# Sliding-window attention and a channel mix on one core: instruction order from a list scheduler, and another order of the first loads

## The chip, the cores and the metric

The kernel runs on one core of one Trainium2 chip. The metric is the device time of one execution in microseconds (us). Each kernel is executed several times and once with the hardware profiler on; "the profile" and "the trace" are of that profiled execution, whose span is about 1.7 us shorter than the device time of the same run. TensorE is called PE below, and its weight loads PEld; VectorE, ScalarE, GpSimd and SyncE appear in the profile as DVE, ACT, POOL and SP.

## The reference

Eight batches of eight heads, 576 positions, 64 channels per head. Attention over a window of 128 positions with a linear distance bias, then a gated two-layer channel mix on the 512 channels. Cut to what matters:

```python
scores = scale * (q @ k.T)                       # per batch and head
mask   = (rel >= 0) & (rel < 128)                # rel = query position - key position
attn   = softmax(where(mask, scores - slope[h] * abs(rel), -1e9))
x      = concat_heads(attn @ v)                  # [8, 576, 512]
xk, xr = mixes of x and x shifted by one position
k      = relu(xk @ w_k) ** 2                     # 512 -> 1024
out    = sigmoid(xr @ w_r) * (k @ w_v)           # 1024 -> 512
```

Note the first matmul of the mix: it sums over all 512 channels, so it needs the attention of all four head pairs for its positions before it can start.

## The kernel before

Work goes by head pair: 32 pairs (8 batches of 4). For one pair PE transposes Q and K, computes the scores, multiplies with V and transposes the result; ScalarE copies the transposes out of PSUM and takes the exponent; VectorE divides by the sums and forms `xk` and `xr`. The channel mix comes in blocks of up to 512 positions, whose pieces ("units") fill PE between the attention steps. The order of the instructions is written by hand (from batch 2 on for PE, SyncE and GpSimd alone; ScalarE and VectorE are then not in the hand-ordered set).

The distance bias can be applied in two ways. For the first two batches (`NEARLY = 2 * G` head pairs) PE adds it into the scores with an extra matmul; later VectorE multiplies the exponent by a mask that was made meanwhile.

```python
    def scores(it, pieces, m0):
        early = it < NEARLY                       # NEARLY = 2 * G: batches 0 and 1
        ...
        if early:
            for hl in range(2):
                nc.tensor.matmul(sa[:, hl, 0:w], lhsT=sid[:, 2 * g + hl],
                                 rhs=dist[:, m0:m0 + w], start=True, stop=False, ...)
        ...                                       # scores, then exp on ScalarE
        if not early:
            nc.vector.tensor_tensor(out=ah, in0=ah,
                in1=mask[:, 2 * g:2 * g + 2, m0:m0 + w], op=ALU.mult)
```

Batch 0 is loaded in two halves of 256 positions in f32 by SyncE and cast on GpSimd, VectorE and ScalarE. The weights follow from GpSimd, which casts while loading, then batch 1:

```python
    load_qk(0, 1, 0); load_qk(1, 1, 0); load_v_block(0, 0); ...   # batch 0, f32, SyncE
    ...
    for i in range(2 * G):                        # i < G: first half of pair i, then second halves
        score(i)
        ...
        if i == G - 1:
            load_w(wk_sb, moe_w_k)
            load_w(wr_sb, moe_w_r)
            load_w(wv_sb, moe_w_v)
        ...
    cast_load_qk(1, 0); cast_load_qk(1, 1); cast_load_tail(1); cast_load_v(1)
    ...
    def first1(c0, fo):                           # first layer of the mix, 256 positions
        mm1(0, c0, c0 + 256, fo)
        if c0 == 256:
            make_mask(range(fo, fo + 1))
```

The softmax here doesn't subtract the row's maximum and nothing guards it: scores larger than these inputs give would overflow.

## Time and profile before

| | before |
|---|---|
| time, median (range) | 266.53 us of the first three runs (266.39 to 267.29) |
| span of the profiled run | 264.8 us |
| PE busy | 239.7 us, 91% |
| first score matmul, first matmul with w_k | 5.24 us, 28.73 us |
| batch 1's first transposes, batch 2's first scores | 40.40 us, 66.61 us |

The head of the page of the kernel before: span, busy time by engine, then the busy share of PE in 40 equal slices in tenths (9 is 90% or more).

```profile
span 264.8 us, 5798 instructions
PE 239.7 (91%) x2272; PEld 144.2 (54%) x2304; DVE 190.1 (72%) x406; ACT 180.0 (68%) x293; POOL 102.9 (39%) x147
PE   4489799977999999999999999999999999999993
```

PE is the busiest engine, and the holes are nearly all in the first ten slices (66 us). But busy is not progress: a matmul at the half clock, or one that stands in the pipeline behind a slow one, counts as busy. The same shows in the table of windows (start and end, length, busy us and instructions of PE, PEld, VectorE, ScalarE, GpSimd; then granted clock, DMA share, GB/s):

```profile
0.00:20.00 20.00, 11.74 (x93) 5.73 (x94) 7.80 (x31) 10.60 (x19) 12.32 (x38) 0.99 0.99 199
20.00:60.00 40.00, 35.56 (x399) 22.14 (x401) 25.48 (x63) 30.96 (x58) 34.32 (x43) 0.96 2.14 165
30.00:40.00 10.00, 9.10 (x70) 6.47 (x69) 6.61 (x21) 7.78 (x24) 6.19 (x8) 1.00 2.25 162
60.00:240.00 180.00, 172.07 (x1680) 105.27 (x1702) 148.39 (x294) 129.03 (x198) 56.26 (x68) 1.00 0.86 90
```

The marks of progress on PE, from the timeline of the kernel before (start, duration, engine, line, operation, output and inputs, count, and in brackets the idle time ahead with what ended it):

```profile
5.24 0.50 PE L242 MATMUL sa<-qk 64*128 64x256 bf16 x4
15.78 0.75 PE L209 MATMUL tp<-ident,cs 128*128 128x128 bf16 x4
28.73 2.34 PE L324 MATMUL ps<-xk,wk_sb 128*128 128x256 bf16 x16
40.40 0.61 PE L196 MATMUL tp<-ident,ldr 128*128 128x128 bf16 x8
```

The first scores start at 5.24 us, the second half of batch 0 at 15.78, the channel mix at 28.73, batch 1 at 40.40. And GpSimd, which issues the casting loads:

```profile
17.23 0.91 POOL L404 DMA_DIRECT2D wv_sb<-in_moe_w_v_dram  x1
32.56 0.87 POOL L110 DMA_DIRECT2D ldr<-in_k_dram  x1 [3.62 <-DMA wv_sb<-in_moe_w_v_dram]
```

The load of w_v is issued at 17.23 us, and GpSimd stands 3.62 us for it before it may issue the last K load of batch 1.

**A count of progress.** I need a measure that does not count slow time as work. I give each matmul its time at full speed, from the trace: 0.216 us for 512 columns (back to back in the steady state), 0.1625 for 384, 0.109 for 256, 0.056 for a 128-column transpose, 0.029 for one of 65 (or 64) columns, and half for the score matmuls of 64 rows, which run in pairs side by side (the two of a pair start 3 to 4 ns apart). Summed over the weight loads, whose records are complete where some matmul records are missing, this is 218.6 us for the kernel before. "Lost" up to a moment is the elapsed time less the work started by then. The kernel before has lost 14.7 us by 20 us, 25.4 by 60, 41.2 by 240 and 46.2 at the end. This is bookkeeping of mine, not a view of the profile.

### The profile page before, as it was taken

The page shows a single profiled execution, that of the slowest core. Times are in us where ns is not written, and L with a number is a line of the kernel's source. Part 1 is how long each engine was busy: PE and PEld are TensorE (multiplying, and loading weights), DVE is VectorE, ACT ScalarE, POOL GpSimd, SP SyncE. Part 2 cuts the span into 40 slices and gives each one's busy share as a digit, 9 for nine tenths or more (in the row PEclk, how much of TensorE's full clock was granted, in tenths as well). Part 3 has the DMA queues.
Part 4 walks back from the last instruction along what each step waited for, and adds up shares of the span by engine and source line. Part 5 has one row for each costly group of instructions (what it writes and reads, how often), then busy time and mean ns, then how long its engine had stood idle before and what let it go on. Part 6 is the DMA issues. An engine that isn't in the chain of part 4 may idle for free.

```text
span 264.8 us, 5798 instructions
## 1 busy us (share of the span) xinstructions
PE 239.7 (91%) x2272; PEld 144.2 (54%) x2304; DVE 190.1 (72%) x406; ACT 180.0 (68%) x293; POOL 102.9 (39%) x147
## 2 busy tenths in 40 slices
PE   4489799977999999999999999999999999999993
PEld 1145664544555755555665755555656655555461
DVE  2259952379758988878887788878778889886241
ACT  5368688873886877876786868866766868626250
POOL 6399389999048066606470249314000000000000
PEclk9997999999999999999999999999999999999999
DMA  6999999999939897939995299919201111031212
GB/s 163 239 197 188 189 155 143 170 144 178 141 23 157 122 87 108 143 57 92 125 145 70 82 129 106 115 42 146 66 30 51 41 42 40 2 119 41 79 42 80
DMA packets 115788, 28.38 MB, mean 107 GB/s; under 512 B 105008, under 2 KB 110640, under 8 KB 115760
## 3 DMA queue, kind: packets, MB, share of 16 engines
q0 software_dynamic: 100608, 15.02, 83.1%
q1 hardware_dynamic: 15152, 12.98, 16.4%
q8 instruction: 18, 0.29, 0.5%
q14 instruction: 10, 0.08, 0.1%
HBM read 33.56 MB, written 9.44 MB: 162 GB/s over the span
## 4 chain that ended last, share of the span: by engine, by line
PE 60%; ACT 13%; DMA 11%; DVE 7%; issue 3%; POOL 3%; SPq 1%; POOLq 0%; DVEq 0%; ACTq 0%
PE pv L353 20%; PE ps L324 16%; PE pr L339 10%; ACT at L245 6%; DMA wv_sb<-in_moe_w_v_dram 6%; PE sa L274 5%; PE tp L196 4%; ACT xt L301 3%; DMA ts<-in_k_dram 3%; DMA vdr<-in_v_dram 2%; PE sa L242 2%; ACT rl L328 2%; PE tp L296 2%; DVE xk L312 2%; ACT qk L199 1%
## 5 line engine op out<-in xcount | busy, mean ns | idle before, releaser
L324 PE MATMUL ps<-xk,wk_sb 128*128 128x256 bf16 (+2 forms) x413 | 70.4, 313 | 2.4 <-ACT rl L328 1.5
L245 ACT ACTIVATE at<-sa 128x1024 bf16<-128x1024 f32 (+1 forms) x68 | 63.7, 984 | 8.0 <-PE sa L242 7.7
L353 PE MATMUL pv<-wv_sb,kk 128*128 128x512 bf16 x271 | 67.7, 379 | 1.2 <-issue 0.5
L328 ACT ACTIVATE rl<-ps 128x256 bf16<-128x256 f32 (+2 forms) x104 | 47.6, 477 | 18.3 <-PE ps L324 13.6
L324 PEld LDWEIGHTS <-wk_sb 128*128 128x128 bf16 x416 | 38.6, 98 | 23.3 <-issue 4.0
L330 DVE TENSOR_TENSOR kk<-rl 128x256 bf16<-128x256 bf16 (+2 forms) x104 | 33.6, 337 | 16.6 <-ACT rl L328 14.4
L116 POOL DMA_DIRECT2D vs<-in_v_dram x28 | 24.8, 908 | 42.4 <-PE sa L274 41.3
L359 DVE SCALAR_TENSOR_TENSOR ot<-rs,pv 128x512 f32<-128x512 bf16 x36 | 24.4, 678 | 23.1 <-PE pv L353 17.5
L353 PEld LDWEIGHTS <-kk 128*128 128x128 bf16 x288 | 26.0, 98 | 26.3 <-DVE kk L330 0.4
L344 ACT ACTIVATE rs<-pr 128x512 bf16<-128x512 f32 x36 | 21.7, 602 | 23.9 <-PE pr L339 23.9
L339 PE MATMUL pr<-wr_sb,xr 128*128 128x512 bf16 x132 | 35.7, 379 | 0.7
L199 ACT COPY qk<-tp 128x1024 bf16<-128x1024 bf16 x28 | 28.4, 1015 | 10.9 <-PE tp L196 10.6
L110 POOL DMA_DIRECT2D ldr<-in_q_dram x28 | 25.1, 917 | 24.3 <-PE tp L196 24.3
L247 DVE TENSOR_TENSOR at<-at,mask 128x1024 bf16<-128x1024 bf16 x48 | 31.0, 684 | 0.8 <-ACT at L245 0.8
L274 PEld LDWEIGHTS <-at 128*128 128x128 bf16 x576 | 22.6, 99 | 12.0 <-issue 7.5
L312 DVE SCALAR_TENSOR_TENSOR xk<-dl,muk_sb,xt 128x576 bf16<-128x576 bf16 (+2 forms) x36 | 27.1, 752 | 1.2
L310 DVE TENSOR_TENSOR dl<-xt 128x576 bf16<-128x576 bf16 (+2 forms) x36 | 15.5, 431 | 16.2 <-ACT xt L301 15.6
L312 DVE SCALAR_TENSOR_TENSOR xr<-dl,mur_sb,xt 128x576 bf16<-128x576 bf16 (+2 forms) x36 | 26.9, 748 | 0.0
L110 POOL DMA_DIRECT2D ldr<-in_k_dram x28 | 24.8, 924 | 4.4 <-DMA wv_sb<-in_moe_w_v_dram 3.6
L282 DVE TENSOR_TENSOR xu<-sa,rc 128x640 bf16<-128x640 f32 x28 | 22.9, 820 | 0.5
L274 PE MATMUL sa<-vs,at 128*128 128x65 bf16 x448 | 18.9, 193 | 3.0 <-ACT at L245 2.6
L242 PE MATMUL sa<-qk 64*128 64x256 bf16 (+1 forms) x264 | 20.8, 265 | 0.6 <-ACT qk L212 0.2
(61 smaller groups left out, 227.7 us busy)
## 6 DMA issues: line engine op xcount, KB each, us to landing
out_dram<-ot SPq DMA_DIRECT2D x36, 256.0 KB, 2.4
ldr<-in_q_dram POOLq DMA_DIRECT2D x28, 128.0 KB, 5.5
ldr<-in_k_dram POOLq DMA_DIRECT2D x28, 128.0 KB, 5.5
vs<-in_v_dram POOLq DMA_DIRECT2D x28, 128.0 KB, 5.5
vdr<-in_v_dram SPq DMA_DIRECT2D x4, 256.0 KB, 5.6
wk_sb<-in_moe_w_k_dram POOLq DMA_DIRECT2D x1, 1024.0 KB, 9.6
wv_sb<-in_moe_w_v_dram POOLq DMA_DIRECT2D x1, 1024.0 KB, 15.0
ldr<-in_q_dram SPq DMA_DIRECT2D x1, 512.0 KB, 5.4
```

The source lines that it names most:

```text
L110: nc.gpsimd.dma_start(out=cb_buf[b % 2][:, i, r], in_=hs[:, :, r])
L199: nc.scalar.copy(out=qk_buf[it % NBUF].rearrange("p t (c r) -> p t c r", r=NF), in_=tp.rearrange("p (t r c) -> p t c r", t=2, r=NF))
L242: nc.tensor.matmul(sa[:, hl, c0:c0 + n], lhsT=kk_, rhs=qq_, start=not early, stop=True, skip_group_check=True)
L245: nc.scalar.activation(out=ah, in_=sa[:, :, 0:w], func=AF.Exp, scale=float(scale))
L247: nc.vector.tensor_tensor(out=ah, in0=ah, in1=mask[:, 2 * g:2 * g + 2, m0:m0 + w], op=ALU.mult)
L274: nc.tensor.matmul(a5[:, hl, t - t0], lhsT=at[:, lo:lo + 128], rhs=vs[:, u, 2 * g + hl, :] if u < NF else tvb[:, 2 * g + hl], start=(u == ...
L312: nc.vector.scalar_tensor_tensor(out=dst[:, g, S * e + c0:S * e + c1], in0=dl[:, 0:c1 - c0], scalar=mu[:, g:g + 1], in1=xp, op0=ALU.mult, ...
L324: nc.tensor.matmul(ps[:, 0:n], lhsT=wk_sb[:, po, 128 * fo:128 * fo + 128], rhs=xk[:, po, c0:c1], start=(po == 0), stop=(po == NPO - 1))
L328: nc.scalar.activation(out=rl[:, 0:n], in_=ps[:, 0:n], func=AF.Relu, scale=RELU_SCALE)
L330: nc.vector.tensor_tensor(out=kk[:, fo, 0:n], in0=rl[:, 0:n], in1=rl[:, 0:n], op=ALU.mult)
L339: nc.tensor.matmul(pr, lhsT=xr[:, po, 128 * c:128 * c + 128], rhs=wr_sb[:, po], start=(po == 0), stop=(po == NPO - 1))
L353: nc.tensor.matmul(pv, lhsT=kk[:, fo, o:o + 128], rhs=wv_sb[:, fo], start=(fo == 0), stop=(fo == NFO - 1))
```

## The change

The intent: put PE's losses at the start and in the steady state away by planning the whole program. A list scheduler in the kernel file holds every operation as a node with engine, assumed duration, dependences and buffers, simulates the engines when the kernel is built, and emits the instructions of all five engines in the order that it finds. The loads change with it: batch 0 comes by casting loads from GpSimd (but for the first half of its first two head pairs), w_k ahead of batch 0's second half, w_v behind batch 1. The bias matmuls are kept for batch 0 only, masks serve from batch 1 on. The diff, cut to its core:

```diff
+class Plan:
+    def add(self, engs, dur, lat, deps, prio, emit=None, need=(), free=()): ...
+    def run(self):        # event simulation: each engine takes its best ready node
+        ...
-    NEARLY = 2 * G
+    NBIAS = 4
+    LAT = {PE: 0.2, ACT: 0.22, DVE: 0.16}
+    def memset(t, v):
+        return dve_op(0.12, lambda e: nc.vector.memset(t, v), [], (0, 0))
+    # v: V blocks 0, 1; 0 1: Q, K of pairs 2, 3 (first half); K: w_k; 2 3: Q, K, second half;
+    # t: last 64 rows; V: V blocks 2, 3; R: w_r; a b c: batch 1; W: w_v   (comment of this text)
+    for what in 'v01K23tVRabcW':
+        load_step(what)
...
-    load_qk(0, 1, 0)
-    load_qk(1, 1, 0)
-    load_v_block(0, 0)
...
+            if part == 0 and g < 2:           # two pairs still come in f32 and are cast
+                cs.append(op((ACT, DVE), ..., copy_any(... half_buf ..., stage ...)))
...
+    with tc.manual_schedule(engines={ENG.PE, ENG.SP, ENG.Pool, ENG.Activation, ENG.DVE}):
+        for n in plan.run():
+            if n.emit is not None:
+                n.emit(n.eng)
```

## The prediction

> **What bounds the kernel now.** TensorE (PE). The page gives PE 91% busy, VectorE 72%, ScalarE 68%; the table of windows gives PE idle 5 us in 80 to 240 us, but about 15 us in 0 to 67. Busy is not useful, so I sum PE work from the timeline of the steady state: 512-column matmuls run back to back at 0.216 us, so the channel mix (9 blocks of 512 rows, 80 matmuls each) is about 154 us. One steady head-pair step takes 0.54 (scores) + 0.76 (attention times V) + 0.45 + 0.38 (transposes) + 0.06 = 2.19 us. From 66.6 us (batch 2 starts) to the last matmul at 260.4 there are 193.8 us for 24 x 2.19 + 136.5 = 189 us of work. So the steady state can give at most about 5 us. The start is another matter: by 66.6 us only batches 0 and 1 and the first 512 rows are done, by my sum about 14.4 + 8.8 + 17 = 40 us of work. 26 us are lost there; the last 4.4 us (last output and its store) stay.
>
> Where those 26 us go: about 15 us idle; 8 bias score pairs of batch 1, each 2 x 512 columns (0.43 us), 3.4 us; the rest slow matmuls (bias pair 0.85 us before 16 us, 0.49 after; granted clock 0.72 in 20 to 25 us). The Trainium skill, "TensorE: Matmul & The Clock Gate", Part 1, says PE starts at half clock until it has been busy for a while; the trace's doubled durations agree. The chain of waits runs through the w_v load (17.2 to 32.3 us): GpSimd idles 3.6 us for it before it may issue batch 1's last K load, whose tail lands at 41.1.
>
> **What changes.** Batch 0: the SyncE loads in f32 and the casts (GpSimd 0.4 us each, VectorE 0.29, ScalarE 0.4) become casting DMAs on GpSimd (0.7 to 0.9 us issue each, about 5.5 us to landing), but for the first two head pairs. w_k is issued at about 7 us instead of 15.6; w_v goes last. Batch 1 loses its bias matmuls (-3.4 us PE) and gains 8 mask multiplies of 0.68 us (+5.5 VectorE). Order on all engines comes from the planner; PSUM and buffers stay about the same.
>
> **How much is on the path.** Saturated loading read about 310 to 350 GB/s of f32 (w_v: 5.2 MB of weights in 15 us). With that, an estimate: w_k lands near 16 us, the second half of batch 0 near 19, w_r 26, batch 1 32 to 36, w_v 43. So PE gets channel-mix work about 12 us earlier and batch 1 about 8 us earlier; the 40 us of work should be done near 53 us instead of 66.6. VectorE, with about 45 us of work in that stretch, is the next limit. Gain 11 to 16 us there, 0 to 3 in the steady state: about 14.
>
> **Predicted: 252 us**, 8 in 10 between 246 and 258. Faster by over 2%: 0.9; within 2%: 0.07; slower: 0.03.
>
> **What would show it.** First w_k matmul near 16 to 18 us (before 28.7); batch 1's transposes at 33 to 36 (before 40.4); batch 2's first scores near 53; no bias matmuls after batch 0; about 187 to 190 us from there to the last matmul; PE busy 94% or more.
>
> **What would make it wrong.** Casting loads with 128-byte pieces too slow (part 1 of batch 0 after 24 us); VectorE saturated until 55 us; the fixed order of ScalarE and VectorE, planned with wrong durations, making PE wait in the steady state, so that the 5 us turn into a loss; a longer time at half clock because PE idles around 10 us.

## The result, and the profile after

| | before | after |
|---|---|---|
| time, median of 4 (range) | 266.46 us (266.28 to 267.29) | 258.89 us (257.67 to 260.09) |
| ratio | | 0.971, 95% interval 0.9657 to 0.9763 |
| span of the profiled run | 264.8 us | 255.9 us |
| PE busy | 239.7 us | 236.9 us |
| work by my count | 218.6 us | 215.2 us |
| lost by 20, 60, 240 us, end | 14.7, 25.4, 41.2, 46.2 | 14.1, 24.3, 35.9, 40.7 |

A ratio is the mean time of one kernel's fast runs over that of the other's of the same rounds, so it is not quite the ratio of the medians. The change is faster by 7.6 us, predicted were 14.5; the time lies just outside the range of 246 to 258. The profiled run of the changed kernel was the fastest of its four. A later repeat (`a18_again`, below) has the span 257.8 us and had lost 14.4, 25.8 and 37.8 us by 20, 60 and 240 us; differences of 1 to 2 us between single profiles mean little.

The head of the page after:

```profile
span 255.9 us, 5768 instructions
PE 236.9 (93%) x2260; PEld 140.0 (55%) x2288; DVE 196.0 (77%) x433; ACT 177.1 (69%) x285; POOL 104.1 (41%) x130
PE   2969986999999999999999999999999999999993
```

The windows after, columns as before:

```profile
0.00:20.00 20.00, 12.46 (x88) 6.41 (x89) 14.92 (x61) 10.80 (x23) 15.71 (x25) 0.91 1.52 146
20.00:60.00 40.00, 35.87 (x456) 23.31 (x458) 32.60 (x73) 32.95 (x52) 33.89 (x41) 1.00 2.16 163
30.00:40.00 10.00, 8.11 (x116) 5.60 (x113) 8.21 (x21) 8.65 (x13) 9.01 (x12) 1.00 2.06 164
60.00:240.00 180.00, 176.97 (x1656) 103.66 (x1679) 143.43 (x289) 128.53 (x200) 54.55 (x65) 1.00 0.86 89
```

In the first 20 us and from 20 to 60 PE is hardly busier than before (12.46 against 11.74 us, 35.87 against 35.56). The clear rise is in the steady state, 176.97 against 172.07. The part from 30 to 40 us is even worse than before, 8.11 against 9.10.

A caution on the granted clock in these tables. A pair of bias matmuls of 384 columns, early and later in the changed kernel, and three windows of it:

```profile
6.07 0.85 PE L468 MATMUL duo<-dist,sid 128*128 128x384 bf16 x2
21.89 0.49 PE L468 MATMUL duo<-dist,sid 128*128 128x384 bf16 x2
0.00:13.10 13.10, 7.66 (x52) 3.43 (x52) 9.26 (x45) 5.36 (x9) 12.09 (x21) 1.00 1.20 138
13.10:16.50 3.40, 1.71 (x23) 0.93 (x23) 2.56 (x9) 3.24 (x9) 0.38 (x1) 1.00 1.79 170
16.50:19.90 3.40, 3.00 (x15) 2.00 (x14) 3.10 (x9) 2.14 (x7) 3.13 (x4) 0.50 2.43 155
```

PE ran at about half speed until 13.1 us, which the column doesn't show; from 16.5 to 19.9 us it was at half clock again. In the repeat full clock came only at 22.2 us, and half clock again from 42.7 to 46.1. So two profiles of one kernel differ in their clock, too.

The marks of progress after:

```profile
6.85 0.50 PE L479 MATMUL duo<-qk 64*128 64x256 bf16 x4
16.37 0.69 PE L618 MATMUL uno<-xk,wk_sb 128*128 128x256 bf16 x3 [0.46 <-ACT xt L455]
20.50 0.61 PE L714 MATMUL uno<-ident,half 128*128 128x128 bf16 x8
32.60 0.61 PE L771 MATMUL uno<-ident,cb 128*128 128x128 bf16 x8
43.96 1.02 PE L651 MATMUL uno<-wv_sb,kk 128*128 128x512 bf16 x3 [0.62 <-DMA wv_sb<-in_moe_w_v_dram]
53.27 0.39 PE L479 MATMUL duo<-qk 64*128 64x256 bf16 x4
```

The channel mix starts 12.4 us earlier (16.37 against 28.73), batch 1 is 7.8 us earlier (32.60 against 40.40) and batch 2's first scores 13.3 us earlier (53.27 against 66.61). That looks like a gain of 12 us. But the first scores are 1.6 us later, and the second half of batch 0 is 4.7 us later (20.50 against 15.78): w_k was loaded in its place. Work was exchanged for work.

GpSimd after:

```profile
16.57 0.89 POOL L344 DMA_DIRECT2D vs<-in_v_dram  x1 [3.08 <-DMA wk_sb<-in_moe_w_k_dram]
44.54 0.88 POOL L365 DMA_DIRECT2D cb<-in_k_dram  x1 [4.06 <-DMA wv_sb<-in_moe_w_v_dram]
```

The wait for w_v has not gone; it stands now ahead of a K load of batch 2, and there is one for w_k besides.

VectorE in the first 6 us, where the changed kernel's first scores are late:

```profile
3.07 0.49 DVE L309 MEMSET tv<- 64x520 bf16 x1 [0.17 <-issue]
4.10 1.03 DVE L446 TENSOR_SCALAR sid<-ident 128x128 bf16<-128x128 bf16 x8
5.06 0.75 DVE L455 CAST half<-stage 128x256 bf16<-128x256 f32 x2
```

The cast that the first transposes need waits behind fills and constants until 5.06 us. The plan gave every fill 0.12 us; this one of 64x520 took 0.49. In the kernel before GpSimd made these fills and the identity (its two fills of 64x520 came at 12.8 and 13.8 us); the change put them on VectorE. The Trainium skill, "VectorE: DVE Perf Modes", section "Zero memsets can be issued as uint32 (trn2)", says that a memset takes one cycle per element whatever the type; the trace agrees in kind: in an experiment below a fill of 1024 bf16 columns took 0.91 us, not much under twice this one of 520, and here one of 128 uint32 columns took 0.17.

And why PE falls back between 30 and 40 us. ScalarE in the changed kernel, and the PE line that waits for it:

```profile
35.87 3.78 ACT L487 ACTIVATE at<-duo 128x1024 bf16<-128x1024 f32 x4
39.50 1.06 ACT L455 COPY qk<-uno 128x1024 bf16<-128x1024 bf16 x1
40.60 0.61 PE L771 MATMUL uno<-ident,cb 128*128 128x128 bf16 x8 [1.11 <-ACT qk L455]
```

Batch 1 has begun, w_v is not there until 43.96 us, and the attention of batch 1 runs at ScalarE's pace: four exponents end to end, then a copy, and PE stands 1.11 us for it. The changed kernel had lost 2.3 us less than before at 30 us (16.2 against 18.5; 17.1 in the repeat), and at 40 us nothing less (20.0 against 20.0; 20.5). That is gained and given back within 10 us.

**Where 7.6 us came from.** The spans differ by 8.9 us: 3.5 us of bias matmuls of batch 1 are gone (16 of 512 columns), 1.1 us are lost less by 60 us (25.4 - 24.3), 4.3 less from 60 to 240 (15.9 against 11.6), next to nothing after that. With the repeat the same terms are 3.5, -0.4 and 3.8, and the spans differ by 7.0. So apart from the bias the start gave between nothing and one microsecond, and the steady state 3.8 to 4.3.

### The profile page after: what moved, and what is told of

It reads as the page before. It is cut to its first block, busy times and chain, and to the rows that moved or that the text cites. A ratio compares the mean times of both kernels' runs of the same rounds, so it can differ in the third digit from the quotient of the medians.

```text
span 255.9 us, 5768 instructions
## 1 busy us (share of the span) xinstructions
PE 236.9 (93%) x2260; PEld 140.0 (55%) x2288; DVE 196.0 (77%) x433; ACT 177.1 (69%) x285; POOL 104.1 (41%) x130
## 4 chain that ended last, share of the span: by engine, by line
PE 78%; POOL 5%; ACT 5%; DMA 4%; DVE 3%; issue 2%; DVEq 0%; ACTq 0%
PE uno L651 25%; PE uno L618 21%; PE uno L637 11%; PE duo L479 7%; PE duo L515 6%; DMA wv_sb<-in_moe_w_v_dram 4%; PE uno L771 4%; PE uno L544 3%; POOL cb L365 3%; ACT at L487 2%; POOL vs L344 1%; ACT rl L625 1%; ACT qk L455 1%; PE duo L468 1%; POOL tv L349 1%
## 5 line engine op out<-in xcount | busy, mean ns | idle before, releaser
L487 ACT ACTIVATE at<-duo 128x1024 bf16<-128x1024 f32 (+2 forms) x68 | 65.8, 980 | 14.1 <-PE duo L479 13.5
L618 PE MATMUL uno<-xk,wk_sb 128*128 128x256 bf16 (+2 forms) x412 | 72.7, 318 | 1.5 <-ACT xt L455 0.5
L651 PE MATMUL uno<-wv_sb,kk 128*128 128x512 bf16 x277 | 71.2, 380 | 1.8 <-issue 0.8
L625 ACT ACTIVATE rl<-uno 128x256 bf16<-128x256 f32 (+2 forms) x104 | 47.3, 477 | 20.7 <-PE uno L618 18.6
L662 DVE SCALAR_TENSOR_TENSOR ot<-rs,uno 128x512 f32<-128x512 bf16 x36 | 24.6, 686 | 22.3 <-PE uno L651 15.9
L365 POOL DMA_DIRECT2D cb<-in_q_dram x28 | 24.6, 903 | 30.2 <-PE uno L771 29.8
L637 PE MATMUL uno<-wr_sb,xr 128*128 128x512 bf16 x131 | 35.8, 379 | 0.6
L344 POOL DMA_DIRECT2D vs<-in_v_dram x32 | 28.5, 909 | 18.7 <-PE duo L515 14.1
L455 ACT COPY qk<-uno 128x1024 bf16<-128x1024 bf16 (+1 forms) x30 | 29.7, 989 | 8.7 <-PE uno L771 8.3
L365 POOL DMA_DIRECT2D cb<-in_k_dram x28 | 24.8, 917 | 5.0 <-DMA wv_sb<-in_moe_w_v_dram 4.1
L479 PE MATMUL duo<-qk 64*128 64x256 bf16 (+1 forms) x264 | 24.2, 263 | 0.1
L637 PEld LDWEIGHTS <-xr 128*128 128x128 bf16 x144 | 13.2, 98 | 13.4 <-issue 0.8
```

The lines of the kernel that those rows point to most:

```text
L365: return [dma(POOL, 256, issue_t(1024), lambda e, r=r: nc.gpsimd.dma_start(out=cb_buf[h.idx][:, i, r], in_=src[:, :, r]), [g]) for r in ra ...
L455: (nc.scalar.copy if e == ACT else nc.vector.tensor_copy)(out=out, in_=in_)
L479: nc.tensor.matmul(sa[:, hl, c0:c0 + n], lhsT=kk_, rhs=qq_, start=not bias, stop=True, skip_group_check=True)
L487: x = op(ACT, act_t(2 * w), [s], prio + (2,), lambda e: nc.scalar.activation(out=ah(), in_=two(hp)[:, :, 0:w], func=AF.Exp, scale=float(sc ...
L618: nc.tensor.matmul(one(hp)[:, 0:n], lhsT=wk_sb[:, po, 128 * fo:128 * fo + 128], rhs=xk_buf[hx.idx][:, po, c0:c1], start=(po == 0), stop=(p ...
L625: a = op(ACT, act_t(n), [s], pr, lambda e, hp=hp, hr=hr: nc.scalar.activation(out=rl_buf[hr.idx][:, 0:n], in_=one(hp)[:, 0:n], func=AF.Rel ...
```

## The experiments

The question is why the start gave so little. My theories at first: (V) from 20 to 60 us VectorE and ScalarE are the limit, because they have taken over masks and have more to do per microsecond; (loads) the weights arrive too late or crowd out the rest; (clock) PE is at half clock while it has little to do; (P) the plan's durations are wrong, so the fixed order makes PE wait; and (M), which came later, several of these together, each hiding the next. In the quoted texts the letters stand for these; any other is described where it is used. Kernels are variants of the changed kernel, except `e7` and `e8`, which are variants of the kernel before. The changed kernel is 258.89 us, 259.25 in its repeat; each ratio is to the kernel before on the same chip. A difference in us is that of the medians, against 259.1, the mean of the changed kernel's two medians.

### Undo the masks in the planned kernel: e1_bias8

```diff
-    NBIAS = 4
+    NBIAS = 8
```

> The changed kernel with the bias matmuls kept for batch 1 (masks from batch 2 on): puts 3.4 us of PE work back and takes 8 mask multiplies (5.5 us of VectorE) away from 35 to 52 us. Theory V (in 33 to 60 us PE waits for VectorE and ScalarE, which a head-pair step of attention keeps 4.4 and 3.6 us against PE's 2.2): the time does not rise, 256.5 to 259.5 us, since PE gets its work back where it was waiting. Theory L (late loads limit the start) and the plain sum of the prediction: bias matmuls cost what they take, 261 to 262.5 us.

Measured: correct, 261.66 us, ratio 0.9803 (0.9766 to 0.9839), +2.6 us on the changed kernel. Work by my count is 3.5 us more, so the bias matmuls seem to cost a little less than they weigh. The masks of batch 1 are worth about 2.6 us in the planned order, of which a microsecond may be the draw of a new plan (see `e4_jitter`).

### Neither bias nor mask for batch 1 (wrong): e2_neither

```diff
-        if bias:
+        if bias or b == 1:
             return s, x
```

> Wrong result on purpose: batch 1 gets neither bias matmuls nor mask multiplies, so 5.5 us of VectorE work are simply gone from the start and nothing else. Theory V: batch 1's attention ends earlier and the kernel is 2 to 4 us faster than the changed kernel (255 to 257). Theory L: VectorE's work is not what the start waits for, within 1 us of the changed kernel (258 to 260).

Measured: 259.48 us, ratio 0.9727 (0.9697 to 0.9758), +0.4 us. Eight multiplies of 0.69 us taken off VectorE gave nothing that can be seen beside a new plan's draw. Theory V in its simple form, which wanted 2 to 4 us, falls: VectorE's mask work is not what limits the start.

### A quarter of w_k and w_r, an eighth of w_v (wrong): e3_lightw

```diff
-            out=dst, in_=src.rearrange("(i p) w -> p i w", p=128)))
+            out=dst[:, 0], in_=src[0:128]))
...
-            n_w["k"] = w_load(wk_sb, moe_w_k, 1600)
+            n_w["k"] = w_load(wk_sb, moe_w_k, 400)      # likewise w_r 200, w_v 200
...
-                        one(hp)[:, 0:n], lhsT=wk_sb[:, po, 128 * fo:128 * fo + 128],
+                        one(hp)[:, 0:n], lhsT=wk_sb[:, 0, 128 * fo:128 * fo + 128],
```

> Wrong result on purpose: only the first 128 rows of each weight matrix are loaded and used for every chunk, so 4.2 of 5.2 MB of weight reads vanish (about 13 us of saturated loading), with the same matmuls. w_k should land near 10 us, w_v near 31 instead of 44, batch 1 near 26. Theory L: 6 to 10 us faster than the changed kernel (249 to 253). Theory V: under 3 us (256 to 259), because VectorE and ScalarE still have the same work.

Measured: 255.66 us (255.52 without the one of its six runs that was slow), ratio 0.9583 (0.9554 to 0.9613), -3.6 us by the fast runs. Batch 0's second half now starts at 16.18 us, and the mix at 20.82: the order of the changed kernel is reversed. w_k landed at 11.1 us instead of 16.3, the last of the second half at 14.6 instead of 19.7. But the work left at 20 us is 209.3 us against 209.3 and 209.5 in the changed kernel's two profiles, and at 50 us 187.0 against 187.3 and 189.2. So even nearly free weights don't make the first 20 us quicker; where the 3.6 us come from later, single profiles that differ by 2 us can't tell. The weight loads are worth about 3.6 us of the whole, give or take the draw of a new plan.

### Almost the same plan: e4_jitter

```diff
-    LAT = {PE: 0.2, ACT: 0.22, DVE: 0.16}
+    LAT = {PE: 0.21, ACT: 0.23, DVE: 0.17}
```

> Control: the planner's latencies after PE, ScalarE and VectorE are 0.01 us longer each, nothing else; the plan is reshuffled a little. All theories: the changed kernel's time within 1 us either way (257.5 to 260.5). More would say that differences of that size between two plans mean nothing.

Measured: correct, 260.38 us, ratio 0.9767 (the changed kernel 0.971 and 0.9731), +1.3 us. A change of 0.01 us in the assumed latencies gives another order and more than a microsecond. It is lost from 60 to 240 us (13.7 us there against 11.6 and 12.0). This is the size below which a comparison of two plans says nothing about its cause. `e1`, `e2`, `e3`, `e12`, `a13`, `a15` and `a16` let the planner run on other numbers and so have a new plan; `e5`, `e6`, `e9`, `a14` and `a17` keep the changed kernel's, `e10` and `e11` that of `e3`.

### Less ScalarE and VectorE work in batches 1 and 2 (wrong): e5_lightv, e9_lightv2

Half-width exponents and copies of the transposed Q and K in batches 1 and 2, no mask multiply in batch 1 and half-width ones in batch 2, in the same order as the changed kernel.

```diff
+        wx = w // 2 if b in (1, 2) else w
-            out=ah(), in_=two(hp)[:, :, 0:w], func=AF.Exp, ...)
+            out=ah()[:, :, 0:wx], in_=two(hp)[:, :, 0:wx], func=AF.Exp, ...)
...
+                if n.eng == DVE and n.t0 > 23.0 and blanks:      # e5 only
+                    nc.vector.memset(at_buf[blanks.pop()][:, 0:2048], 1.0)
```

> Wrong result on purpose, the plan and the order of every instruction kept: in batches 1 and 2 ScalarE's exponentials and Q/K copies do half their columns, batch 1's mask multiplies are left out and batch 2's halved (two buffers are filled once instead). Between 33 and 65 us this takes about 11 us from ScalarE and 8 us from VectorE. Theory V in its wider form (PE waits in 30 to 60 us for the throughput of ScalarE and VectorE): 4 us or more faster than the changed kernel, 252 to 255. Rival, theory C (the time of the start is lost before 20 us, in the latency of the first head pairs and at half clock, and the rest in the switching between small groups): within 2 us, 257 to 260.

Measured: 259.52 us, ratio 0.9758, +0.4 us. The experiment was flawed: the two fills that initialise the buffers took 1.76 us each on VectorE, and PE stood for them, as the timeline of e5_lightv shows:

```profile
32.57 0.34 PE L546 MATMUL uno<-ident,xu 128*128 128x128 bf16 x3 [3.31 <-DVE xu L524]
```

`e9_lightv2` has no fills, and narrows an instruction only where the buffer was already written in full.

> e5 again without its flaw (there two 1.8 us fills of buffers on VectorE, put in to avoid unset data, held PE up for 3.3 us at 29 to 32 us). Wrong result on purpose, same plan and order: half-width exponentials (where the buffer was filled before) and Q/K copies in batches 1 and 2, no mask multiplies in batch 1, half ones in batch 2. Theory V: 252 to 255. Theory C: 257 to 260.

Measured: 257.55 us, ratio 0.9678 (0.9654 to 0.9703), -1.6 us. The work of ScalarE and VectorE alone is worth one to two microseconds.

### Warm PE with dummy matmuls: e6_warm

```diff
+        def heat(n, w):
+            for _ in range(n):
+                nc.tensor.matmul(uno[3][:, 0:w], lhsT=warm[:, 0:128], rhs=warm[:, 0:w], ...)
+        heat(6, 512)
...
+                if n.eng == PE and n.t0 < 15.0:
+                    heat(1, 256)
```

> The changed kernel, with matmuls on a constant tile that nothing reads: 6 of 512 columns before the first transpose (1 to 4 us) and one of 256 columns after each PE group until about 15 us, so that PE reaches full clock some 7 us sooner. Theory C: the slow groups of 0 to 20 us (4.6 us of excess) shrink below 2 us, and the kernel gains 1.5 to 3.5 us (255.5 to 257.5). Theory V: the start waits for other engines anyway, within 1 us (258 to 260).

Measured: correct, 259.67 us, ratio 0.976, +0.6 us: no gain. The timeline of e6_warm shows when the clock came:

```profile
1.46 2.74 PE L800 MATMUL uno<-warm 128*128 128x512 bf16 x6 [1.46 <-DVE warm L796]
9.37 0.39 PE L800 MATMUL uno<-warm 128*128 128x256 bf16 x1
9.89 0.28 PE L800 MATMUL uno<-warm 128*128 128x256 bf16 x1
```

Six matmuls of 512 columns took 2.74 us, half speed; full speed came at 9.9 us instead of 13.1 and 22.2 in the changed kernel's two profiles, and half clock was back from 16.7 to 20.1. The fill of the dummies' tile also put the first V load back by 0.5 us. The first matmul with w_k then came at 16.71, not earlier: it waits for w_k and for `xk`. My reading is that a faster PE alone does not shorten a chain that is made of loads, ScalarE and VectorE, and that the dummies lengthen it where they stand in it.

### Masks in the kernel before: e7_b_masks

```diff
-    NEARLY = 2 * G
+    NEARLY = G
...
-        if c0 == 256:
+        if c0 == 0:
             make_mask(range(fo, fo + 1))       # and copy_mask ahead of batch 1
```

> The kernel before with one part of the change: no bias matmuls after batch 0, the masks made during the first 256 rows and multiplied from batch 1 on. Removes 3.4 us of PE work, adds 5.5 us of VectorE in 43 to 62 us. If the bias matmuls' time counts in full, as the complement of the first experiment suggests (2.5 to 3.4 us): 263 to 264.5. If VectorE takes it back (theory V): 266 to 268.

Measured: correct, 266.33 us, ratio 1.001 (0.9977 to 1.0044). Work fell by 3.5 us, and the loss by 60 us rose by 3.7 (29.1 against 25.4; the profiled run was the slowest of the six, 268.9 us). The matmuls that were taken off PE turned into waits for ScalarE and VectorE, one for one.

### w_v behind batch 1 in the kernel before: e8_b_wvlate

```diff
             load_w(wr_sb, moe_w_r)
-            load_w(wv_sb, moe_w_v)
...
     cast_load_v(1)
+    load_w(wv_sb, moe_w_v)
```

> The kernel before with one part of the change: w_v is loaded after batch 1. In the chain of waits of before, batch 1's loads stood behind w_v until 41 us. Prediction's theory (that chain is the start's limit): batch 1's first transposes at 33 to 36 us instead of 40.4 only where PE's fixed order allows it; 2 to 4 us faster (262.5 to 264.5). Rival (PE has channel-mix work then, and does it in its fixed order): within 1 us of before, or slower by the later w_v (266 to 269).

Measured: correct, 271.22 us, ratio 1.0176 (1.015 to 1.0201), +4.9 us. In the hand-written order the next piece of work is the second layer, and PE stands for w_v:

```profile
45.88 1.89 PE L353 MATMUL pv<-wv_sb,kk 128*128 128x512 bf16 x4 [3.37 <-DMA wv_sb<-in_moe_w_v_dram]
```

### Light weights and warm PE: e10_warmw; with light ScalarE and VectorE as well: e11_warmwv (both wrong)

The edits of `e3` and `e6` together, and of `e3`, `e6` and `e9` together.

> Wrong result on purpose: the light weight loads of e3 and the warm-up matmuls of e6 together. In e3 PE stayed at half clock to 21 us, in e6 PE stood waiting for w_k and for batch 0's second half; each hid the other. Theory M (several limits of the start stand at nearly the same place: clock, loads, the chain of the first head pairs; taking one away lets the next one bind): 2 us or more faster than e3, 250.5 to 253.5. Theory C (the in-order chain through ScalarE and VectorE alone): e3's time within 1 us, 254.5 to 256.5.

> Wrong result on purpose: light weight loads, warm-up matmuls and the lighter ScalarE and VectorE of e9, all together. Theory M: 248 to 251.5, that is about what the prediction had expected of the start once all three limits are gone. If it stays at 254 or more, none of the three matters and the fixed order or PE's own work is what the start costs.

Measured: 254.97 us, ratio 0.9558 (0.9542 to 0.9574), 0.6 us under `e3`'s fast runs; and 253.29 us, ratio 0.9508 (0.9483 to 0.9534), 5.8 us under the changed kernel. Theory M expected at least 2 us for the first pair and 248 to 251.5 for all three; neither was reached. From 20 to 60 us the three together do help. The windows of e11_warmwv (the dummies count as busy in the first one):

```profile
0.00:20.00 20.00, 16.21 (x131) 8.81 (x132) 14.48 (x59) 11.21 (x23) 18.52 (x29) 1.00 1.65 132
20.00:60.00 40.00, 38.35 (x531) 27.28 (x528) 31.67 (x77) 30.56 (x62) 39.47 (x48) 1.00 2.38 152
```

PE is 38.35 us busy from 20 to 60 instead of 35.87, and the work left at 60 us is 175.9 instead of 179.5 and 180.9. But the work left at 20 us is 208.9 against 209.3 and 209.5: light weights and dummy matmuls do not move the first 20 us by more than half a microsecond. The lighter ScalarE and VectorE can't be seen there, for they begin with batch 1, whose first transposes come at 30.75 us. Nor was PE warm early in this profile: full clock came at 12.4 us. It was in e10_warmw, at 5.1 us, and there the loss by 20 us was 13.4 us against 14.2 in `e3`, and by 60 us 23.9 in both.

### w_v early in the planned kernel: e12_wvearly

```diff
-    for what in 'v01K23tVRabcW':
+    for what in 'v01K23tVRWabc':
```

> The changed kernel with one part undone: w_v is loaded before batch 1, the planner told so. In the kernel before, moving w_v behind batch 1 alone cost 4.8 us, because its PE order reached for w_v at 42 us. If the move only pays together with an order planned for it: 260 to 263 here (batch 1 some 7 us later). If it never mattered: 257.5 to 260.5.

Measured: correct, 261.28 us, ratio 0.9811 (0.9782 to 0.984), +2.2 us. The second layer starts at 31.1 us, batch 1 at 37.5. This kernel had lost less than the changed one by 40 us (17.1 against 20.0, and 20.5 in the repeat), and a little more by 80 (29.8 against 27.5, and 29.3). An early lead was given back here too. My reading is that with batch 1's attention late there was later too little channel mix to put in between; that was not tested.

### The chain of the first head pairs: a14_delay, a13_head, a17_defer

What `e11` did not touch is batch 0's first loads and, but for PE's clock, the chain of the first head pairs: load, cast, transpose, copy, scores, exponent, product with V, division, transpose, copy, `xk`. First, lengthen it: the same order, and two fills on VectorE early on.

```diff
+                if n is n_ident:
+                    for t in (2, 3):
+                        nc.vector.memset(at_buf[t][:, 0:1024], 1.0)
```

> The changed kernel, correct, same plan and order, with two useless fills of about 0.9 us each on VectorE after the identity is made, so that the first casts come about 1.8 us later and the loads do not. If the chain of the first head pairs sets the start, 1.2 to 1.8 us slower than the changed kernel (260 to 261). If it has slack against the loads, under 0.8 us (258 to 259.7).

Measured: correct, 261.27 us, ratio 0.9815 (0.9793 to 0.9837), +2.2 us. PE at the start of a14_delay:

```profile
7.74 0.61 PE L714 MATMUL uno<-ident,half 128*128 128x128 bf16 x4 [3.38 <-DVE half L455]
8.92 0.50 PE L479 MATMUL duo<-qk 64*128 64x256 bf16 x4
```

The first scores are 2.07 us later (8.92 against 6.85), the first w_k matmul comes at 18.91 (16.37), the second half at 23.54 (20.50), and the kernel is 2.2 us longer. Against the repeat, whose full clock came about as late as here (22.2 and 23.6 us), all three are 2.07 to 2.08 us later (6.84, 16.84, 21.47).

But the experiment is flawed: against the expectation, the loads did move. GpSimd in the changed kernel, then in a14_delay:

```profile
2.09 1.91 POOL L344 DMA_DIRECT2D vs<-in_v_dram  x2
4.17 1.90 POOL L344 DMA_DIRECT2D vs<-in_v_dram  x2 [2.15 <-DVE vs L309]
```

The first V load waits for VectorE's fill of its buffer, which stood behind the two new fills, and the casting loads that follow it on GpSimd were issued about 2.1 us later with it. w_k landed at 17.57 us, against 16.28 and 15.51 in the changed kernel's two profiles, the last of the second half at 21.54 against 19.71 and 19.06. So a delay of chain and loads together goes into the total one for one; that the chain alone would is not shown.

Then shorten it. `a13_head` puts the fills and constants that aren't needed at first behind the first copy, and lets the plan run again:

```diff
-    for t in range(NV):
-        blank.append(memset(tv_buf[t][64:128], 0.0))
+    def set_late(y):                              # y: the first copy of Q and K
+        for t in range(NV):
+            late.append(memset(tv_buf[t][64:128], 0.0, [y], 0.5))
...                                                # likewise the other fills, sid 4 to 7, two copies of dist
```

> The changed kernel, correct; on VectorE the clearing of buffers that are not needed yet, four of the eight scaled identities and two of the three copies of the distances come after the first head pair's Q/K copy, not before the first casts (in the changed kernel they held the first cast until 5.06 us, planned with 0.12 us for fills that took 0.49). First scores near 5.3 us instead of 6.85. If the chain of the first head pairs sets the start: 1 to 2 us faster than the changed kernel (256.5 to 258). If it has slack (loads of w_k and of batch 0's second half come later anyway): within 1 us (258 to 260).

Measured: correct, 261.12 us, ratio 0.9812 (0.9791 to 0.9834), +2.0 us. First scores at 6.26 us, 0.6 earlier, but the new plan differs elsewhere. It starts the masks ahead of work that PE needs, and the first matmul with w_k comes at 23.83 us instead of 16.37:

```profile
17.88 0.40 PE L554 MATMUL uno<-ident,xu 128*128 128x128 bf16 x2 [2.32 <-ACT mask L757]
23.83 0.60 PE L628 MATMUL uno<-xk,wk_sb 128*128 128x256 bf16 x4
```

So it says nothing about the chain. `a17_defer` keeps the plan and defers the same instructions on VectorE alone:

```diff
+        later = blank[2 * NA + NV:] + n_sid[4:] + [n_copy[c0] for c0, _ in DSEG[1:]]
         for n in plan.run():
+            if copies < 2 and n in later:
+                put_off.append(n)
+                continue
```

> The changed kernel, correct, with the same plan and the same order on PE, ScalarE, GpSimd and SyncE; on VectorE alone the clearing that nothing needs yet, sid 4 to 7 and two copies of the distances are put behind the first two Q/K copies. First cast on VectorE near 4 us instead of 5.06. If the chain of the first head pairs alone sets the start, as the delay suggests: 0.8 to 1.3 us faster than the changed kernel (257.3 to 258.2). If the loads stand right behind it (w_k landed at 16.7 us, the second half of batch 0 at 20.5): within 0.6 us.

Measured: correct, 258.91 us, ratio 0.9719 (0.9702 to 0.9736), the changed kernel's time (259.25). VectorE at the start of a17_defer:

```profile
4.18 0.29 DVE L456 CAST half<-stage 128x256 bf16<-128x256 f32 x1 [1.08 <-DMA stage<-in_q_dram]
5.26 0.38 DVE L456 CAST half<-stage 128x256 bf16<-128x256 f32 x1 [0.78 <-DMA stage<-in_k_dram]
5.55 1.27 DVE L456 COPY qk<-uno 128x512 bf16<-128x512 bf16 x2
```

The copy that the first scores need stands behind the cast for the second pair, and that one waits 0.78 us for its load. So the scores came at 6.66 us, only 0.2 earlier. The Trainium skill, "TensorE: Matmul & The Clock Gate", Part 1, "Engine queue depths", says that VectorE takes its queue strictly in order; this trace agrees. The chain was hardly shortened, and whether shortening it would pay stays open.

### Better durations in the plan: a15_calib, a16_headcalib

```diff
-        dur = sum(max(n / 2400 + .0025, .03) for _, _, n in pieces) + ...
+        dur = 0.1 + sum(max(n / 2400 + .0025, .03) for _, _, n in pieces) + ...
...                     # +0.05 for each group of transposes or AV matmuls, +0.02 for first-layer groups
```

`a16_headcalib` has the edit of `a13_head` besides.

> The changed kernel, correct, with the planner's PE durations raised by what the trace shows a group to cost beyond its columns (0.1 us for scores, 0.05 for transposes and for attention times V, 0.02 for a channel-mix block). Theory P (wrong durations spoil the order): 2 us or more faster (under 257). Otherwise within the 1.5 us that the jitter run showed between plans (257.4 to 260.4).

> Both: the shortened chain of the first head pairs and the raised PE durations. If both are causes, 254.5 to 257; if neither is, 257.5 to 260.5.

Measured: correct, 264.38 us, ratio 0.9934 (0.99 to 0.9968), and 264.03 us, ratio 0.9915 (0.9888 to 0.9941): both 4.9 us worse than the changed kernel (one of `a15`'s six runs was slow; its fast ones have a median of 264.01). The plan ends PE's work at about 237.5 us and the trace at 251, so its durations are too short, and yet longer ones made it worse. Theory P falls in this form. The order that the change ships is one of many, and its other constants (the priorities, and the assumed lead of the attention over the mix) go with its durations.

### The changed kernel again: a18_again

No edit.

> Control: the changed kernel once more, unchanged. 257.5 to 260, ratio 0.967 to 0.975 to the kernel before. If it lies outside, verdicts of 1 to 2 us above are to be read with that much more doubt.

Measured: 259.25 us (258.85 to 259.59), ratio 0.9731 (0.9713 to 0.9749). The change is reproduced. No correct variant was clearly faster.

## Why the prediction was right or wrong

| predicted | measured |
|---|---|
| 252 us, 246 to 258 | 258.89 us |
| first w_k matmul near 16 to 18 us | 16.37 |
| batch 1's transposes at 33 to 36 | 32.60 |
| batch 2's first scores near 53 | 53.27 |
| no bias matmuls after batch 0 | so |
| 187 to 190 us from there to the last matmul | about 198 (53.3 to 251.1) |
| PE busy 94% or more | 93% |
| 40 us of work done near 53 us instead of 66.6 | 60.4, in the repeat 62.4 |
| gain in the start 11 to 16 us, in the steady state 0 to 3 | 3.1 to 4.5 (3.5 of it bias) and 3.8 to 4.3 |

**Right: direction, mechanism of the loads, and the markers.** The loads arrived about as estimated (w_k at 16.3 us for 16, the second half at 19.7 for 19, w_r at 25.4 for 26, batch 1 at 32.3 to 39.1 for 32 to 36, w_v at 43.9 for 43), and three of the markers were met within a microsecond. The Trainium skill, "DMA: Bandwidth & Descriptors", section "SWDGE vs HWDGE vs iDMA", says that only GpSimd can issue loads that cast. The trace agrees with that as far as it goes: all casting loads of both kernels are on GpSimd's queue. In the prediction their issue was costed with 0.7 to 0.9 us each, which they took, and the second half of batch 0 did not come after 24 us, the limit that I had named.

**Wrong: "the 40 us of work should be done near 53 us instead of 66.6."** This is the step that failed. What the kernel before had done by 66.6 us (39.4 us by my count, 3.5 of it bias of batch 1) the changed one had done, without that bias, at 60.4 us: 6.2 us earlier, 3.5 of them bias, so 2.7 for all the rest (0.7 in the repeat) where about 10 were predicted. I had taken the marker for the work: batch 2's scores did begin at 53 us, but a part of the first 512 rows' mix was still to do, and it was done by about 65. The error shows in the next row of the table as well: from 53.3 us on there were not 189 but about 198 us to go.

Behind it lies a false inference: "PE gets channel-mix work about 12 us earlier and batch 1 about 8 us earlier", hence the work is done 10 us earlier. Two things were left out.

- Loading w_k first puts half of batch 0 back. The mix came 12.4 us earlier, that half 4.7 us later, and the work left at 20 us is 209.3 against 213.4, which apart from the 3.5 us of bias is 0.6 us less.
- The first 20 us, in which both kernels lose 14 us, are not limited by when w_k and the second half of batch 0 come: with both some 5 us earlier (`e3`) the loss by 20 us was the same, and with PE at full clock from 5.1 us besides (`e10`) it was 0.8 us less. What is left is the first loads of batch 0 and the chain of the first head pairs through ScalarE and VectorE. `a14` put back both at once, no run lightened ScalarE or VectorE in batch 0, and I did not manage to shorten the chain. So which of them limits the start stays open.

From 20 to 60 us the prediction named VectorE as "the next limit". That was too simple. Weights alone are worth 3.6 us (`e3`), ScalarE and VectorE alone 1.6 (`e9`), the masks of VectorE alone nothing (`e2`), the clock alone nothing (`e6`), and all together 5.8 (`e11`). The single gains add up to 5.2, so within the draw of a plan these limits do not hide one another; theory M falls, and the larger part of the loss lies in none of them. From 30 to 40 us PE waits for ScalarE's exponents of batch 1, as the lines above show.

**Mis-sized the other way: the steady state.** I gave it 0 to 3 us and put 1 into the sum, and it gave 3.8 to 4.3 (lost from 60 to 240 us: 15.9 before, 11.6 and 12.0 after). That hid about 3 us of the miss in the start, by luck. The fear that wrong durations would turn the 5 us there into a loss did not come true. The planned order is good for the steady state, though its times drift from the chip's by about 14 us: from 80 to 240 us the three kernels in the hand-written order lost 12.3 to 13.0 us (before, `e7`, `e8`), the seventeen profiles of planned ones 7.7 to 10.9, whatever their loads. Whether that is PE's order or ScalarE's and VectorE's, which are now planned too, was not tried apart.

**The bias term was right in size.** 3.4 us predicted, 3.5 of work gone. But `e7` shows that the same edit is worth nothing in the hand-written order, and `e1` that undoing it in the planned one costs about 2.6 us. The late w_v is the same: -2.2 us in the planned order (`e12`), +4.9 in the hand-written one (`e8`). These two parts of the change pay only in an order made for them.

**Open:** what limits the first 20 us, the first loads or the first chain; the casting loads of batch 0 were not tried alone; and why better durations make a worse plan.

## What to carry to other kernels

When a load moves forward, ask what moves back, and predict with the work done by a time, not with the time at which some later stage begins: a marker can come 13 us earlier with 3 us gained. A limit at a start-up can be looked for by lengthening one chain a little and seeing whether the end moves by as much, but only when the trace shows that nothing else came later with it: here the loads did. Taking away weight loads and half clock moved the first 20 us by less than a microsecond, and so told where their limit is not. And an order from a planner is a draw: before a part of such a change is judged, run a plan with trivially different numbers; here that alone moved the time by 1.3 us, and well-meant ones by 4.9.

## What the Trainium skill lacked or had wrong

- "DMA: Bandwidth & Descriptors", the section on one DMA from GpSimd, calls the generation of descriptors small. With the 1024 pieces of 128 bytes of a Q, K or V load it was not: GpSimd took 0.89 to 0.92 us for each (0.75 to 0.76 for the last rows of Q and K, half as many; medians of the changed kernel), 28.5 us of the span for its 32 V loads alone. The page's latency table has about 1 us to the first byte and puts it down to this work, which fits; it gives no figure for the issue time by number of pieces.
- The same section's fit of time to bytes (2.0 us and a share by bandwidth) is for one DMA alone. In a full queue the loads of 128 KB took a median of 5.5 us before and 5.9 to 6.7 after from issue to landing, and the halves of batch 0 9.4 us. The page has nothing for a load behind others.
- "TensorE: Matmul & The Clock Gate", Part 1, has full clock after about 3.4 us of sustained work. With 2.74 us of gapless dummies from 1.46 us and one more after each group, full clock came at 5.1 us in `e10_warmw`, at 9.9 in `e6_warm` and only at 12.4 in `e11_warmwv`. Half clock came back for 3.4 us after 3.4 us in which PE was busy 1.71 us in the changed kernel and 1.78 in its repeat, in many short pieces and without a gap of more than 1.11 us. The traces agree that sustained work is needed; how much idle time within a stretch puts full clock off or ends it, the page does not say for gaps of about a microsecond.
- No page treats how a fixed order planned from assumed durations behaves on the chip. Here the plan ended 14 us before the chip did, and plans from nearly equal numbers differed by 1.3 to 4.9 us.
